# Loading the weights of a quad's four pieces one piece per row tile instead of all eight loads at once

## The chip, the cores and the metric

The kernel runs on one core of a Trainium2 chip. The metric is the device time of one execution in microseconds; the median of three runs is compared. The engines are PE (TensorE), DVE (VectorE), ACT (ScalarE), POOL (GpSimd) and SP, which here does nothing but read registers and issue DMAs.

## The reference, cut to what matters

A gated linear attention over 4 batches, 8 heads, 768 steps and 48 channels gives 3072 rows of 384 numbers. Each row then goes to one of 8 experts, picked by the largest of 8 logits, and comes back scaled by its softmax weight.

```python
for t in range(S):
    state = f[:, :, t, :, None] * state + einsum('bhd,bhe->bhde', k[:, :, t], v[:, :, t])
    y[:, :, t] = einsum('bhd,bhde->bhe', q[:, :, t], state)
x = y as (3072, 384)
logits = x @ w_gate                       # (3072, 8)
expert_idx = argmax(logits, axis=1)
for e in range(8):                        # rows of expert e
    y[rows] = maximum(x[rows] @ w1[e], 0) @ w2[e]      # 384 -> 1024 -> 384
out = gate_w[:, None] * y
```

All of it is fp32. One expert's weights are `w1` (384 x 1024) and `w2` (1024 x 384), 1536 KB each.

## The kernel before, in words

**First stage (to about 178 us).** Twelve units of attention are computed in a software pipeline. Finished rows, together with their token number and gate weight, are scattered by POOL into a table `xs` in device memory, where every expert owns a region. Near its end the first row tiles of experts 0 and 1 (`EARLY = 2`) are already worked through.

**Second stage, row tiles (lines 735 to 829).** Every expert gets three tiles of 128 rows (`TILES = 3`); two are done early, which leaves 22 tiles in the list `order` (line 305): two each of experts 0 and 1, three each of experts 2 to 7. Below, "tile i" is entry i of this list, counted from 0, and "turn i" the pass of the loop that works it. For a tile, `widen` (line 256) does 48 matmuls with `w1t` at line 263, ACT and DVE apply the ReLU, and `narrow` (line 275) does 16 matmuls with `w2t` at line 277; DVE scales by the gate weight (line 284) and POOL scatters the result to `out`. Between the two, `turn` (line 247) transposes a later tile's rows by three matmuls at line 250. Thus PE's order within a turn is: widen tile i, transpose tile i + 2, narrow tile i.

**Second stage, quads.** An expert that has more than 384 rows spills into pieces of `T = 32` rows each. Pieces of different experts are gathered four at a time into a quad, a tile of 128 rows in which every piece needs its own expert's weights. There are two quads (`QUADS = 2`). Which rows and which expert a piece has is known only at run time; `share` writes the slots into `sloti`, and SP reads each into a register (`value`, line 746). `load_quad` (line 740) issues four `qrow` loads (line 751) and then, per piece, one load of `w1` into `qw1` and one of `w2` into `qw2` (line 755); the page gives both the name `qw`. Both quads use the same buffers (`qp` has one of each). The dictionary at line 809 places them: quad 0 is worked in turn 11 and quad 1 in turn 21, the last. In such a turn the quad is transposed and widened ahead of the tile (`widen_quad`, line 770) and narrowed behind it (`narrow_quad`, line 798).

**What sets the order.** The stage is under a manual schedule: every engine executes its instructions in the order in which the program text issues them. PE, DVE, ACT, POOL and SP are all named in it. All loads of this stage are SP's, on one DMA queue. In turn i SP gets, in this order:
- `ahead("load", i + 5)` at line 813: row tile i + 4, one load of 200 KB (line 244). There are six row buffers; the load waits until tile i - 2 has been scaled at line 284.
- in a turn with a quad, after the quad has been narrowed: `load_quad` of the next quad (line 827). Its `qrow` loads wait for the scaling of the quad before.
- after the last tile of expert e: the weights of expert e + 2 (line 829), `w1t` at line 300 and `w2t` at line 302. There are two buffers of each, so they wait until that last tile has been widened and narrowed.

`load_quad(0)` stands ahead of the loop (line 810). Weights 2 are issued in turn 1 and first used by tile 4, weights 3 in turn 3 (tile 7), weights 6 in turn 12 (tile 16) and weights 7 in turn 15 (tile 19).

Of the kernel before, what the change touches and what calls it, by code (L numbers as in the profile page):

```python
# [111 lines left out]
def kernel(  # L112
# [129 lines left out]
    def load_rows(row):  # L242
        xt = rowp.tile([128, ROW], F32, name="xrow")
        nc.sync.dma_start(xt, xs[row] if isinstance(row, slice) else xs[ds(row, C)])
        return {"x": xt}
# [10 lines left out]
    def widen(x, w, hp, blocks):  # L256

        if "hT" not in x:
            x["hT"] = ep.tile([128, NF, C], F32, name="hT")
        for b in blocks:  # L260
            g, f = divmod(b, 4)
            for j in range(KD):
                nc.tensor.matmul(  # L263
                    hp[g][:, f, :],
                    lhsT=w[0][:, j, b * 128 : b * 128 + 128],
                    rhs=x["xT"][:, j, :],
                    start=j == 0,
                    stop=j == KD - 1,
                )
            if b == 3:  # L270
                nc.scalar.activation(x["hT"][:, 0:4], hp[0], AF.Relu)  # L271
            elif b == 7:
                nc.vector.tensor_scalar(x["hT"][:, 4:8], hp[1], 0.0, None, op0=OP.max)  # L273
# [8 lines left out]
    def put(x, yp, group):  # L282
        ysb = ep.tile([128, DM], F32, name="ysb")
        nc.vector.tensor_scalar(ysb, yp, x["x"][:, GATE : GATE + 1], None, op0=OP.mult)  # L284
        scatter(out, x["dst"], ysb, N - 1, group)
# [12 lines left out]
    def load_weights(e):  # L298
        w1t = wpool.tile([128, KD, F], F32, name="w1t")
        nc.sync.dma_start(w1t, moe_w1[e].rearrange("(k p) f -> p k f", p=128))  # L300
        w2t = wpool.tile([128, NF, DM], F32, name="w2t")
        nc.sync.dma_start(w2t, moe_w2[e].rearrange("(f p) d -> p f d", p=128))
        weights[e] = w1t, w2t
# [5 lines left out]
    def ahead(what, count):  # L309
        for e, t in order[done[what] : count]:  # L310
            if what == "load":
                tiles[e, t] = load_rows(slice(first[e] + t * C, first[e] + t * C + C))
            yield tiles[e, t]
        done[what] = max(done[what], min(count, len(order)))
# [405 lines left out]
    def tile_pools(st):  # L720
        pool = lambda name, bufs: st.enter_context(tc.tile_pool(name=name, bufs=bufs, space=PSUM))
        psh, pse, psz = pool("psh", 4), pool("pse", 2), pool("psz", 2)

        def banks():
            return [psh.tile([128, 4, C], F32, tag="hps", name="hps") for g in range(2)]

        def turn_late(x):
            turn(x, pse.tile([128, KD, C], F32, name="etp"))

        def narrow_late(x, w, group="out"):  # L730
            narrow(x, w, psz.tile([128, DM], F32, name="yps"), group)

        return banks, turn_late, narrow_late, psz

    with ExitStack() as st:
        banks, turn_late, narrow_late, psz = tile_pools(st)
        qp = st.enter_context(tc.tile_pool(name="qp", bufs=1))
        st.enter_context(tc.manual_schedule(engines=ordered))

        def load_quad(q):  # L740

            x = qp.tile([128, ROW], F32, name="qrow")
            w1 = qp.tile([128, 4, KD, F], F32, name="qw1")
            w2 = qp.tile([128, 4, NF, DM], F32, name="qw2")

            def value(k, g, most):
                at = sloti[0:1, k, 4 * q + g : 4 * q + g + 1]
                return nc.values_load(at, [mybir.EngineType.SP], min_val=0, max_val=most)

            for g in range(4):  # L750
                nc.sync.dma_start(x[g * T : g * T + T], xs[ds(value(0, g, NONE), T)])
            for g in range(4):
                e = value(1, g, E - 1)
                for w, src, k in ((w1, moe_w1, KD), (w2, moe_w2, NF)):
                    nc.sync.dma_start(  # L755
                        w[:, g], src[ds(e, 1)].rearrange("o (k p) f -> p (o k) f", p=128)
                    )
            return {"x": x, "w": (w1, w2)}

        def pieces():  # L760
            return [(g, slice(g * T, g * T + T)) for g in range(4)]

        def widen_quad(x):

            hp = banks()
            hq = qp.tile([128, 2, 4, C], F32, name="hq")
            for b in range(2):
                for j in range(KD):
                    for g, r in pieces():
                        nc.tensor.matmul(  # L770
                            hp[b][r].rearrange("p f c -> p (f c)"),
                            lhsT=x["xT"][:, j, r],
                            rhs=x["w"][0][:, g, j, b * 512 : b * 512 + 512],
                            start=j == 0,
                            stop=j == KD - 1,
                            skip_group_check=True,
                        )
                if b == 0:
                    nc.scalar.activation(hq[:, b], hp[b], AF.Relu)
                else:  # L780
                    nc.vector.tensor_scalar(hq[:, b], hp[b], 0.0, None, op0=OP.max)
            x["hq"] = hq

        def turn_quad(x):
            tp = banks()
            x["hT"] = qp.tile([128, NF, C], F32, name="hqT")
            for b in range(2):
                for f in range(4):
                    nc.tensor.transpose(tp[b][:, f], x["hq"][:, b, f], ident)
                (nc.scalar.copy if b == 0 else nc.vector.tensor_copy)(  # L790
                    x["hT"][:, 4 * b : 4 * b + 4], tp[b]
                )

        def narrow_quad(x):
            yp = psz.tile([128, DM], F32, name="yps")
            for f in range(NF):
                for g, r in pieces():
                    nc.tensor.matmul(  # L798
                        yp[r],
                        lhsT=x["hT"][:, f, r],  # L800
                        rhs=x["w"][1][:, g, f],
                        start=f == 0,
                        stop=f == NF - 1,
                        skip_group_check=True,
                    )
            put(x, yp, "out")


        quads = {len(order) // 2: 0, len(order) - 1: 1}
        quad = load_quad(0)  # L810
        for i, (e, t) in enumerate(order):
            w = weights[e]
            list(ahead("load", i + 5))
            if i in quads:
                turn_late(quad)
                widen_quad(quad)
            hp = banks()
            widen(tiles[e, t], w, hp, range(NF))
            if i in quads:
                turn_quad(quad)  # L820
            for x in ahead("turn", i + 3):
                turn_late(x)
            narrow_late(tiles[e, t], w)
            if i in quads:
                narrow_quad(quad)
                if quads[i] + 1 < QUADS:
                    quad = load_quad(quads[i] + 1)
            if t == TILES - 1 and e + 2 < E:
                load_weights(e + 2)

    todo = nc.values_load(fixi[0:1, 0:1], min_val=0, max_val=1)
    with tc.If(todo > 0):
# [79 lines left out]
        with ExitStack() as st:  # L912
            banks, turn_late, narrow_late, psz = tile_pools(st)
            with tc.For_i(0, E) as e:
# [10 lines left out]
                with tc.For_i(e * REGION + skip, rows_to, C) as at:  # L925
                    x = load_rows(at)
# [59 lines left out]
```

## Time and profile before

| what | us |
|---|---|
| median of 3 runs | 475.91 |
| the three runs | 472.23, 475.91, 477.03 |
| the profiled execution | 474.65 |
| its span, first to last instruction | 472.8 |
| PE busy in the span | 416.1 |
| mean granted clock of TensorE, share of full | 0.959 |

The times of single instructions below come from the profiled execution and count from the start of its span. In the timelines, a line is one instruction or a run of the same ones; the bracket at its end gives the idle time of the engine before it and what ended it. A timeline of SP shows its DMA issues; the transfer itself goes on after the issue.

### The profile page before, as it was taken

The page shows a single profiled execution, that of the slowest core. Times are in us where ns is not written, and L with a number is a line of the kernel's source. Part 1 is how long each engine was busy: PE and PEld are TensorE (multiplying, and loading weights), DVE is VectorE, ACT ScalarE, POOL GpSimd, SP SyncE. Part 2 cuts the span into 40 slices and gives each one's busy share as a digit, 9 for nine tenths or more (in the row PEclk, how much of TensorE's full clock was granted, in tenths as well). Part 3 has the DMA queues.
Part 4 walks back from the last instruction along what each step waited for, and adds up shares of the span by engine and source line. Part 5 has one row for each costly group of instructions (what it writes and reads, how often), then busy time and mean ns, then how long its engine had stood idle before and what let it go on. Part 6 is the DMA issues. An engine that isn't in the chain of part 4 may idle for free.

```text
span 472.8 us, 8470 instructions
## 1 busy us (share of the span) xinstructions
PE 416.1 (88%) x3580; PEld 336.6 (71%) x3581; DVE 159.4 (34%) x325; ACT 123.5 (26%) x172; POOL 113.7 (24%) x133
## 2 busy tenths in 40 slices
PE   0498798989898989999999999999990799999993
PEld 0488697979797877777777888576870588887471
DVE  4776748686654341211111111121110111111110
ACT  4778577878653200000000000010000001000010
POOL 4555465667461320000000110001000000000001
PEclk9979889999799999999999999999996799999997
DMA  8999755799712144999924515401899954000000
GB/s 312 406 382 383 296 215 214 268 358 377 288 71 71 71 138 166 394 397 393 389 84 148 183 36 186 168 0 40 293 398 387 357 175 180 18 17 18 17 2 20
DMA packets 42445, 98.29 MB, mean 208 GB/s; under 512 B 3440, under 2 KB 27301, under 8 KB 42400
## 3 DMA queue, kind: packets, MB, share of 16 engines
q1 hardware_dynamic: 38496, 87.48, 50.6%
q0 software_dynamic: 3200, 9.64, 5.3%
q8 instruction: 29, 0.48, 0.4%
q10 hardware_dynamic: 704, 0.56, 0.4%
q14 instruction: 16, 0.13, 0.1%
HBM read 81.43 MB, written 16.63 MB: 207 GB/s over the span
## 4 chain that ended last, share of the span: by engine, by line
PE 78%; ACT 7%; SPq 4%; DMA 4%; DVE 3%; issue 2%; POOL 1%; POOLq 0%; ACTq 0%
PE hps L263 23%; PE yps L277 22%; PE s L409 5%; PE xp L514 5%; PE yt L453 5%; SPq L755 4%; DMA xrow<-xs 3%; PE dp L469 3%; PE yt L433 3%; PE hps L770 2%; PE yps L798 2%; PE yp L277 2%; PE s L263 2%; ACT L389 2%; PE etp L250 2%
## 5 line engine op out<-in xcount | busy, mean ns | idle before, releaser
L263 PEld LDWEIGHTS hps<-xT,w1t 128*128 128x128 f32 x1056 | 121.1, 192 | 7.3 <-issue 2.3
L263 PE MATMUL hps<-xT,w1t 128*128 128x128 f32 x1056 | 121.8, 275 | 0.0
L277 PE MATMUL yps<-w2t,hT 128*128 128x384 f32 x352 | 118.3, 490 | 0.0
L277 PEld LDWEIGHTS yps<-w2t,hT 128*128 128x128 f32 x352 | 65.8, 192 | 41.3 <-issue 0.9
L161 POOL DMA_INDIRECT out_dram<-ysb,dst x26 | 25.3, 972 | 272.6 <-DVE ysb L284 272.6
L271 ACT ACTIVATE hT<-hps 128x512 f32<-128x512 f32 x22 | 13.1, 597 | 237.8 <-PE hps L263 237.8
L273 DVE TENSOR_SCALAR hT<-hps 128x512 f32<-128x512 f32 x22 | 15.2, 692 | 106.2 <-PE hps L263 101.1
L284 DVE TENSOR_SCALAR ysb<-yps,xrow 128x384 f32<-128x384 f32 x22 | 13.6, 618 | 94.3 <-PE yps L277 94.3
L409 PE MATMUL s<-q,k 64*128 64x128 f32 x384 | 29.8, 315 | 15.4 <-POOL last L392 15.4
L409 PEld LDWEIGHTS s<-q,k 64*128 64x128 f32 x384 | 27.3, 223 | 15.9 <-POOL last L392 15.0
L366 DVE TENSOR_TENSOR_SCAN r<-f,cap 128x1032 f32<-128x1032 f32 (+1 forms) x13 | 28.7, 2208 | 12.4 <-POOL f L359 12.4
L412 DVE COPY_PREDICATED at<-mpack,s 128x1024 f32<-128x1024 uint8 x24 | 30.2, 1309 | 5.8 <-PE s L409 5.7
L161 POOL DMA_INDIRECT xs<-xr,posi x24 | 24.1, 1006 | 24.4 <-DVE xr L232 7.5
L378 POOL TENSOR_TENSOR k<-k,r 128x1024 f32<-128x1024 f32 (+1 forms) x13 | 26.4, 2027 | 2.5 <-DVE r L366 2.4
L250 PE MATMUL etp<-fpack,xrow 128*128 128x128 f32 x72 | 12.2, 281 | 15.6 <-DMA xrow<-xs 15.2
L514 PE MATMUL xp<-fpack,ys 128*128 128x104 f32 x192 | 24.3, 280 | 0.7 <-ACT ys L494 0.7
L433 PE MATMUL yt<-at,v 128*64 128x128 f32 x384 | 24.1, 279 | 0.0
L514 PEld LDWEIGHTS xp<-fpack,ys 128*128 128x128 f32 x192 | 22.3, 191 | 2.2 <-ACT ys L494 1.0
L453 PE MATMUL yt<-q,state 48*48 48x128 f32 x320 | 22.5, 298 | 0.0
L433 PEld LDWEIGHTS yt<-at,v 128*64 128x64 f32 x384 | 21.2, 139 | 1.3 <-issue 0.2
L453 PEld LDWEIGHTS yt<-q,state 48*48 48x48 f32 x320 | 19.6, 133 | 1.8 <-issue 1.7
L424 PE MATMUL kp<-fpack,k 128*128 128x128 f32 x96 | 14.8, 291 | 6.5 <-ACT kn L425 3.9
(107 smaller groups left out, 364.6 us busy)
## 6 DMA issues: line engine op xcount, KB each, us to landing
qw<-in_moe_w_dram SPq DMA_DIRECT2D x16, 1536.0 KB, 9.0
w1t<-in_moe_w_dram SPq DMA_DIRECT2D x8, 1536.0 KB, 12.2
w2t<-in_moe_w_dram SPq DMA_DIRECT2D x8, 1536.0 KB, 7.9
xs<-pad SPq DMA_DIRECT2D x8, 800.0 KB, 11.1
v<-in_vu_dram SPq DMA_DIRECT2D x12, 512.0 KB, 6.9
f<-in_fu_dram SPq DMA_DIRECT2D x11, 516.0 KB, 7.9
k<-in_ku_dram SPq DMA_DIRECT2D x11, 512.0 KB, 11.5
q<-in_qu_dram SPq DMA_DIRECT2D x11, 512.0 KB
```

Of the source, the lines that this page charges most:

```text
L161: ins = nc.gpsimd.indirect_dma_start(out=dst, out_offset=bass.IndirectOffsetOnAxis(ap=idx, axis=0), in_=src, in_offset=None, bounds_check= ...
L250: nc.tensor.transpose(tp[:, j, :], x["x"][:, j * 128 : j * 128 + 128], ident)
L263: nc.tensor.matmul(hp[g][:, f, :], lhsT=w[0][:, j, b * 128 : b * 128 + 128], rhs=x["xT"][:, j, :], start=j == 0, stop=j == KD - 1,)
L277: nc.tensor.matmul(yp, lhsT=x["hT"][:, f, :], rhs=w[1][:, f, :], start=f == 0, stop=f == NF - 1)
L366: nc.vector.tensor_tensor_scan(x["r"][:, part].rearrange("p s c -> p (s c)"), x["f"][:, part].rearrange("p s c -> p (s c)"), cap[:, part]. ...
L378: nc.gpsimd.tensor_tensor(k, k, r[:, :, 1:CR], op=OP.mult)
L409: nc.tensor.matmul(ps[:, h, p], lhsT=x["k"][r, s], rhs=x["q"][r, s], start=True, stop=True)
L412: nc.vector.copy_predicated(x["at"][:, a].rearrange("p h s c -> p (h s) c"), _bc(causal, 1, SEG), ps.rearrange("p h s c -> p (h s) c"),)
L433: nc.tensor.matmul(x["yt"][r, a, p], lhsT=x["v"][:, a, 2 * p + h], rhs=x["at"][:, a, h, p], start=p == 0, stop=x["old"] is None, skip_grou ...
L453: nc.tensor.matmul(x["yt"][r, a, p], lhsT=x["old"][r, HP * a + p], rhs=x["q"][r, HP * a + p], start=False, stop=True, skip_group_check=True,)
L514: nc.tensor.matmul(xp[:, p], lhsT=x["ys"][:, a, p], rhs=wx[:, p], start=True, stop=True)
L755: nc.sync.dma_start(w[:, g], src[ds(e, 1)].rearrange("o (k p) f -> p (o k) f", p=128))
```

## The change

`load_quad` becomes a generator. Its first step allocates the quad's tiles and issues the four `qrow` loads; each further step issues the two weight loads of one piece. The loop takes the first step where `load_quad` was called before. It takes one further step in every turn that has no quad, after the turn's row load at line 813 and ahead of the turn's matmuls, until the four pieces are used up. Quad 0's pieces so belong to turns 0 to 3 and quad 1's to turns 12 to 15. No load, no matmul and no buffer is added or dropped.

```diff
--- before.py
+++ after.py
@@ -749,13 +749,14 @@
 
             for g in range(4):
                 nc.sync.dma_start(x[g * T : g * T + T], xs[ds(value(0, g, NONE), T)])
+            yield {"x": x, "w": (w1, w2)}
             for g in range(4):
                 e = value(1, g, E - 1)
                 for w, src, k in ((w1, moe_w1, KD), (w2, moe_w2, NF)):
                     nc.sync.dma_start(
                         w[:, g], src[ds(e, 1)].rearrange("o (k p) f -> p (o k) f", p=128)
                     )
-            return {"x": x, "w": (w1, w2)}
+                yield None
 
         def pieces():
             return [(g, slice(g * T, g * T + T)) for g in range(4)]
@@ -807,10 +808,13 @@
 
 
         quads = {len(order) // 2: 0, len(order) - 1: 1}
-        quad = load_quad(0)
+        coming = load_quad(0)
+        quad = next(coming)
         for i, (e, t) in enumerate(order):
             w = weights[e]
             list(ahead("load", i + 5))
+            if i not in quads:
+                next(coming, None)
             if i in quads:
                 turn_late(quad)
                 widen_quad(quad)
@@ -824,7 +828,8 @@
             if i in quads:
                 narrow_quad(quad)
                 if quads[i] + 1 < QUADS:
-                    quad = load_quad(quads[i] + 1)
+                    coming = load_quad(quads[i] + 1)
+                    quad = next(coming)
             if t == TILES - 1 and e + 2 < E:
                 load_weights(e + 2)
```

## Rows read from the trace of the kernel before

**Rows 1.** The page: its first line.
```profile
span 472.8 us, 8470 instructions
```

**Rows 2.** The page: 40 slices of 11.8 us; busy tenths, granted clock, GB/s.
```profile
PE   0498798989898989999999999999990799999993
...
PEclk9979889999799999999999999999996799999997
...
GB/s 312 406 382 383 296 215 214 268 358 377 288 71 71 71 138 166 394 397 393 389 84 148 183 36 186 168 0 40 293 398 387 357 175 180 18 17 18 17 2 20
```

**Rows 3.** The chain that ended last, in order of time: start us, us, what.
```profile
316.17 0.33 PE etp L250 x3
...
333.95 0.63 SPq L755
...
354.66 14.58 DMA xrow<-xs
369.37 0.87 PE etp L250 x3
370.25 6.20 PE yps L277 x16
...
382.13 5.16 PE yps L277 x16
```

**Rows 4.** Timeline of PE: start us, us, instructions, [idle before <-releaser].
```profile
337.84 5.52 PE L263 MATMUL hps<-xT,w1t 128*128 128x128 f32 x48
...
348.68 5.52 PE L263 MATMUL hps<-xT,w1t 128*128 128x128 f32 x48
369.37 0.87 PE L250 MATMUL etp<-fpack,xrow 128*128 128x128 f32 x3 [15.17 <-DMA xrow<-xs]
...
376.28 5.52 PE L263 MATMUL hps<-xT,w1t 128*128 128x128 f32 x48
```

**Rows 5.** Windows: stretch and length, busy us per engine, PEclk, DMA share, GB/s.
```profile
337.80:348.60 10.80, 10.80 (x68) 8.73 (x67) 1.83 (x4) 0.60 (x1) 0.97 (x1) 1.00 1.04 391
...
369.30:376.20 6.90, 6.83 (x19) 4.31 (x20) 0.62 (x2) 0.00 (x0) 0.00 (x0) 0.79 1.04 385
```

**Rows 6.** Timeline of SP's DMA issues around the second quad: start us, us, issue.
```profile
327.67 3.63 SPq L751 DMA_DIRECT2D qrow<-xs  x4
332.14 22.48 SPq L755 DMA_DIRECT2D qw<-in_moe_w_dram  x8
354.66 6.17 SPq L244 DMA_DIRECT2D xrow<-xs  x1
360.93 0.62 SPq L300 DMA_DIRECT2D w1t<-in_moe_w_dram  x1
```

**Rows 7.** DMA issues: form, KB each, median us to landing.
```profile
qw<-in_moe_w_dram SPq DMA_DIRECT2D x16, 1536.0 KB, 9.0
w1t<-in_moe_w_dram SPq DMA_DIRECT2D x8, 1536.0 KB, 12.2
...
xrow<-xs SPq DMA_DIRECT2D x24, 200.0 KB, 8.3
```

**Rows 8.** Timeline of SP's DMA issues around the first quad.
```profile
182.65 22.95 SPq L755 DMA_DIRECT2D qw<-in_moe_w_dram  x8
205.70 6.51 SPq L244 DMA_DIRECT2D xrow<-xs  x1
212.30 0.71 SPq L300 DMA_DIRECT2D w1t<-in_moe_w_dram  x1
```

**Rows 9.** Timeline of PE: starts of tiles 2 and 4 and of both quads.
```profile
205.41 5.52 PE L263 MATMUL hps<-xT,w1t 128*128 128x128 f32 x48
...
227.11 5.52 PE L263 MATMUL hps<-xT,w1t 128*128 128x128 f32 x48
...
304.38 5.36 PE L770 MATMUL hps<-qw,xT 128*32 128x512 f32 x48 [0.85 <-DVE dst L254]
...
442.38 5.36 PE L770 MATMUL hps<-qw,xT 128*32 128x512 f32 x48 [0.85 <-DVE dst L254]
```

## The prediction

> **What bounds the kernel now.** I read the page first. In the 40 slices (11.8 us each) the second half of the run has a PE digit of 9 nearly everywhere, with one hole: slice 30 shows 0 and slice 31 shows 7, the granted clock falls to 6 and 7 tenths in the same two slices, and the transfers run at 387 and 357 GB/s meanwhile [rows 2]. So the second half is bound by TensorE except for one place where TensorE stands still and the DMA queue works at full rate.
>
> The chain of waits in order of time says what that place is. It leaves the matmuls at 333.95 us for SP's queue at line 755 (the quad's weight loads), stays there until 354.66, goes on to the load of a row tile that takes 14.58 us to land, and comes back to PE at 369.37 with the transposes of that row tile [rows 3]. PE's own timeline gives the hole from its side: tile 14's widening starts at 348.68, and the next instruction, the transposes at line 250, idles 15.17 us for `xrow` [rows 4]. SP's timeline gives it from the third side: four `qrow` loads from 327.67, eight `qw` loads from 332.14 for 22.48 us, and only then, at 354.66, one `xrow` load [rows 6]. That is row tile 16, asked for in the loop's turn 12 (loads run to i + 4), transposed in turn 14 (transposes run to i + 2). It lands 354.66 + 14.58 = 369.24 us. Its issue begins the moment the eighth `qw` load is issued: SP works in program order, and the row stands behind the whole quad.
>
> **The hole's price.** Between tile starts: 348.68 − 337.84 = 10.84 us for an undisturbed tile, 376.28 − 348.68 = 27.60 us for the one with the hole [rows 4]. The excess is 16.76 us. Its parts: 15.17 us idle; the transposes then take 0.87 instead of 0.33 us (+0.54) and the narrowing 6.20 instead of 5.16 us (+1.04) [rows 3], because the granted clock is 0.79 in 369.3 to 376.2 us against 1.00 at 337.8 to 348.6 us [rows 5]; before it fell PE had stood still. 15.17 + 0.54 + 1.04 = 16.75. Bounds for the slow restart: 0 to 1.58 us; I take it all, since the clock stays at 1.00 (2.4 GHz) over the tile that has no idle time before it.
>
> **The change part by part, second quad.** Nothing is added or dropped: sixteen `qw` loads of 1536 KB and sixteen register reads stay. Only SP's order changes. At 331.3 us (327.67 + 3.63) SP has issued the four `qrow` loads [rows 6]. New order: row 16, piece 0, weights of expert 6 (two loads, the second waiting for tile 12's narrowing, which ends at 337.84 where tile 13 starts [rows 4]), row 17, piece 1, row 18, piece 2, row 19, piece 3, weights 7, row 20. Row 16 now has only the `qrow` loads ahead. Even if it needed the 14.58 us that it took behind the whole quad, it would land at about 346, and it is due when tile 14's widening ends, at 354. So the wait goes.
>
> What is late next? I price the queue by the slower of two rates. From 332.14 to row 16's landing at 369.24 are 37.1 us for eight loads of 1.573 MB and the row's 0.205 MB, 12.79 MB [rows 6, 7]: 2.90 us per MB. (The granted rate in the window at 337.8 is 391 GB/s, 2.56 us per MB [rows 5].) Tiles start every 10.85 us after 348.68; a tile's transposes come 5.36 us after its start. Counting from 332.14, with 3.15 MB for a piece or an expert:
> - row 17: 6.7 MB, lands 351.6; due in turn 15 at 364.9; 13 us to spare.
> - weights 6: before row 17; due 370.4.
> - row 18: 10.05 MB, 361.3; due 375.7.
> - row 19: 13.4 MB, 371.0; due 386.6.
> - weights 7: 19.7 MB, 389.3; due 402.9. They were issued only after tile 15 released their buffer, in either order.
> - row 20: 19.9 MB, 389.9; due in turn 18 at 397.4; 7.5 us to spare, the tightest of all (14 us at 391 GB/s).
> - piece 3: 16.6 MB, 380; due at the quad's turn, 442.38 − 16.76 = 425.6 [rows 9].
> None is late at either rate, so I take 0 for all of them.
>
> **First quad.** Eight `qw` loads from 182.65 delay row 5 to 205.70 and weights 2 to 212.30 [rows 8], yet tile 4, the first to use weights 2, starts on time at 227.11 [rows 9]. There is no hole to gain. What the change moves: pieces 0 and 1 go out at once; then SP stops at weights 2, whose buffers tile 1 frees between its widening and 205.4 (tile 2's start, [rows 9]); pieces 2 and 3 queue behind that wait, with row 6, row 7 and weights 3. Weights 2 are issued 7 us or more earlier than before, weights 3 still wait for tile 3. Pieces 2 and 3 start near 206 and, 6.3 MB at 2.90, are in by 225; the quad is due at 304.38 [rows 9]. Cost between 0 and 0: the cover is 79 us. If that cover were gone, each us late would be one us on PE.
>
> SP gets no new wait, but the pieces stand behind old ones (a row buffer, the weight buffers); behind them only rows and experts' weights wait, counted above. POOL's queue carries the output scatters and none of it moves.
>
> The Trainium skill speaks against the change: its page "DMA: Bandwidth & Descriptors" (Rules for kernel authors) says to issue a DMA early, compute, and wait late. By it, holding back six of eight loads could only lose; the rows agree for what is due soon (row 16 was the transfer issued too late) and give the pieces 45 us or more of slack, so here the rule works for the rows and costs the pieces nothing. By the rule alone the sum would be no gain and a loss wherever something ends up behind the late pieces; that is rival 3.
>
> **Sum.** The profiled execution took 474.65 us, 472.8 of it span [rows 1]. 474.65 − 16.76 = 457.9. The median of the three runs, 475.91, is 1.26 us above this execution; the same subtraction from it gives 459.15. The forecast is halfway: 458.5 us, a gain of about 3.6%.
>
> **Rivals.**
> 1. *The wait shrinks but comes back behind a later row.* Row 20, behind weights 7 and piece 3, needs better than (397.4 − 332.14) / 19.9 = 3.28 us per MB (305 GB/s). At 3.6 us per MB it lands at 403.8 and costs 6.4 us and a slow restart of up to 1.6: about 466. For it: this is the longest stretch with the queue full, 57 us without a break. Against: both rates read above are better.
> 2. *The change does not do what it says.* Nothing paces the pieces but SP's order and its buffers, so pieces 1 to 3 go out in a bunch around 338 to 350, and if row 16 were still held, for instance by the `qrow` loads' wait for the first quad's output, the hole would stay: 475.9. Against it: those four loads are through at 331.3, 23 us before the row is due.
> 3. *Slower: rows and weights 7 starve behind the late pieces.* One mechanism, at row 20 in turn 18: what used to be loaded in one stretch with nothing behind it but one row now shares the queue with every row and two experts. Below (397.4 + 16.8 − 332.14) / 19.9 = 4.12 us per MB (243 GB/s) the new hole outweighs the old one; at 4.5 us per MB (222 GB/s) row 20 lands at 421.7, 24.3 us late, and the time is 458.5 + 24.3 + 1.6 = 484. For it: rates of 71 to 215 GB/s do stand in the slices. Against: those are slices where little was asked for; where a quad loads, slices show 387 to 398 [rows 2].
>
> **How the numbers follow.** Forecast 87%, rival 1 6%, rival 2 4%, rival 3 3%. A measurement of this kernel can tell about 1% from no change: 471.2 is the line. Faster by over 1%: 87 + 6 = 93%; within 1%: 4%; slower: 3%. The three runs of before spread from 472.23 to 477.03, that is −3.7 and +1.1 about the median; around 458.5 that, and the bounds of the restart (0 to 1.6), give 454.5 on the low side. The high side takes the 459.15, the spread, and the near part of rival 1: 463. Left outside: most of rivals 1 to 3 and a little of the forecast, under 2 in 10.
>
> **What would show it right or wrong.** Right: SP's timeline after 327 shows `qrow`, then one `xrow`, then `qw` loads in pairs with `xrow` and weight loads between; PE has no idle entry for `xrow` in 340 to 400; tiles start every 10.85 us throughout; the slices have no 0 and the granted clock no dip there; SP line 755 and `xrow` leave the chain. Wrong: an idle entry at line 250 for `xrow` in a turn from 15 to 18, or at line 263 for weights 6 or 7, or at line 770 for a piece; a gain short of 15 us with no such entry would mean that the tile period itself grew under the longer transfer traffic.

## The result and the profile after

The changed kernel takes 454.75 us, median of four runs (454.02 to 458.41), against 476.47 for the kernel before beside it; the ratio is 0.957, with a 95% interval of 0.948 to 0.966. The forecast was 458.5 us, range 454.5 to 463.0. Two experiments below contain one execution each that was over 1.5% slower than the fastest of its kernel (466.29 and 485.08 us, at a mean granted clock of 0.953 and 0.936); the ratios leave these two out, and one of the kernel before (478.69 us).

The page of the changed kernel, its first line and three rows of the 40 slices, answers to [rows 1, 2]:

```profile
span 452.2 us, 8471 instructions
...
PE   0488898989898998999999999999999999999992
...
PEclk9979889999899999999999999999999999999998
...
GB/s 307 407 379 389 365 226 224 225 352 385 376 61 94 88 83 89 396 354 385 389 355 20 209 157 19 259 94 1 42 313 395 394 391 370 25 17 19 17 2 21
```

The slice with 0 and the slice with 7 are gone, and with them the 6 and 7 of the granted clock. Slices 30 to 33, where most of the second quad's weights come in, hold 370 to 395 GB/s under a PE that shows 9. The dips of the clock that are left (slices 2, 4, 5 and 10, counted from 0) lie in the first stage, but for the 8 of the last slice.

PE's timeline of the tile stage (start, length, instructions) answers to [rows 4, 9]:

```profile
179.86 5.52 PE L263 MATMUL hps<-xT,w1t 128*128 128x128 f32 x48
...
300.52 5.36 PE L771 MATMUL hps<-qw,xT 128*32 128x512 f32 x48 [0.85 <-DVE dst L254]
...
333.98 5.52 PE L263 MATMUL hps<-xT,w1t 128*128 128x128 f32 x48
...
344.82 5.52 PE L263 MATMUL hps<-xT,w1t 128*128 128x128 f32 x48
350.18 0.49 PE L250 MATMUL etp<-fpack,xrow 128*128 128x128 f32 x3
...
355.67 5.52 PE L263 MATMUL hps<-xT,w1t 128*128 128x128 f32 x48
...
421.77 5.36 PE L771 MATMUL hps<-qw,xT 128*32 128x512 f32 x48 [0.85 <-DVE dst L254]
```

Tiles 13, 14 and 15 start at 333.98, 344.82 and 355.67, 10.84 and 10.85 us apart; none of the tiles' lines carries an idle entry. The transposes of row 16 (350.18) take 0.49 us in the timeline, like any others. The chain through the same place no longer leaves PE; it answers to [rows 3]:

```profile
344.99 5.36 PE hps L263 x48
350.35 0.33 PE etp L250 x3
350.67 5.16 PE yps L277 x16
```

The windows over tiles 14 and 15 (columns as in [rows 5]) have the clock at 1.00 while the queue moves 390 GB/s or more:

```profile
344.80:355.70 10.90, 10.90 (x69) 8.75 (x68) 1.83 (x4) 0.60 (x1) 0.97 (x1) 1.00 1.05 390
355.70:366.50 10.80, 10.80 (x68) 8.70 (x67) 1.83 (x4) 0.60 (x1) 0.97 (x1) 1.00 1.05 395
```

SP's DMA issues around the second quad answer to [rows 6]:

```profile
323.81 3.63 SPq L751 DMA_DIRECT2D qrow<-xs  x4
327.49 0.42 SPq L244 DMA_DIRECT2D xrow<-xs  x1
328.73 1.02 SPq L756 DMA_DIRECT2D qw<-in_moe_w_dram  x2
329.86 0.65 SPq L300 DMA_DIRECT2D w1t<-in_moe_w_dram  x1
334.17 0.38 SPq L302 DMA_DIRECT2D w2t<-in_moe_w_dram  x1
334.60 6.86 SPq L244 DMA_DIRECT2D xrow<-xs  x1
342.24 1.09 SPq L756 DMA_DIRECT2D qw<-in_moe_w_dram  x2
343.43 6.62 SPq L244 DMA_DIRECT2D xrow<-xs  x1
350.83 1.36 SPq L756 DMA_DIRECT2D qw<-in_moe_w_dram  x2
...
359.70 2.26 SPq L756 DMA_DIRECT2D qw<-in_moe_w_dram  x2
...
370.44 6.74 SPq L244 DMA_DIRECT2D xrow<-xs  x2
```

Four `qrow` loads, then row 16 at 327.49, and only then piece 0; the last line is rows 20 and 21. The row is issued 22.7 us before it is due at 350.2; before, it was issued at 354.66 for 354. The first quad's issues answer to [rows 8]:

```profile
178.86 0.97 SPq L756 DMA_DIRECT2D qw<-in_moe_w_dram  x2
180.71 0.36 SPq L244 DMA_DIRECT2D xrow<-xs  x1
181.84 3.17 SPq L756 DMA_DIRECT2D qw<-in_moe_w_dram  x2
196.26 0.38 SPq L300 DMA_DIRECT2D w1t<-in_moe_w_dram  x1
...
203.54 1.17 SPq L756 DMA_DIRECT2D qw<-in_moe_w_dram  x2
```

Pieces 0 and 1 go out at once; SP then waits for tile 1's weight buffer until 196.26 and comes to piece 2 at 203.54. Counted from the start of tile 0, weights 2 go out after 16.4 us (196.26 − 179.86) instead of 28.6 (212.30 − 183.72).

Call the stretch from tile 0's widening to the start of the last scaling of quad 1 the tile stage. It was 464.69 − 183.72 = 280.97 us and is 444.08 − 179.86 = 264.22 us. The difference, 16.75 us, is the hole as it was priced (16.76). The profiled executions differ by 474.65 − 454.02 = 20.63 us; the other 3.86 us are in hand before tile 0 starts (183.72 against 179.86), in a stage whose program text the change does not touch. Most experiments below are about these two numbers.

### The profile page after: what moved, and what is told of

The parts are those of the page before. It is cut to its first block, busy times and chain, and to the rows that moved or that the text cites. A ratio compares the mean times of both kernels' runs of the same rounds, so it can differ in the third digit from the quotient of the medians.

```text
span 452.2 us, 8471 instructions
## 1 busy us (share of the span) xinstructions
PE 410.8 (91%) x3580; PEld 332.3 (74%) x3581; DVE 159.1 (35%) x325; ACT 123.8 (27%) x172; POOL 114.3 (25%) x133
## 4 chain that ended last, share of the span: by engine, by line
PE 86%; ACT 7%; DVE 3%; issue 2%; POOL 1%; DMA 1%; POOLq 0%; ACTq 0%
PE hps L263 26%; PE yps L277 25%; PE s L409 5%; PE xp L514 5%; PE yt L453 5%; PE dp L469 3%; PE yt L433 3%; PE s L263 2%; PE hps L771 2%; PE yps L799 2%; PE yp L277 2%; ACT L389 2%; PE kp L424 2%; PE etp L250 2%; ACT f L389 2%
## 5 line engine op out<-in xcount | busy, mean ns | idle before, releaser
L409 PE MATMUL s<-q,k 64*128 64x128 f32 x384 | 28.1, 303 | 15.5 <-POOL last L392 15.5
L409 PEld LDWEIGHTS s<-q,k 64*128 64x128 f32 x384 | 25.8, 212 | 15.9 <-POOL last L392 15.1
L397 DVE TENSOR_TENSOR q<-q,f 128x1024 f32<-128x1024 f32 (+1 forms) x13 | 14.8, 1144 | 15.0 <-ACT f L389 14.9
```

The costliest lines, as they stand in the source:

```text
L409: nc.tensor.matmul(ps[:, h, p], lhsT=x["k"][r, s], rhs=x["q"][r, s], start=True, stop=True)
```

## Experiments

Diffs are against the changed kernel unless another is named. "One look" is a single time beside a profile.

**Second quad alone.** The first quad's pieces go out at once, as before.

```diff
         quad = next(coming)
+        list(coming)
         for i, (e, t) in enumerate(order):
```

> Only the second quad's weights are spread over turns; the first quad's eight loads go out at once, as before. Theory (the whole gain is the hole for row 16 in the second quad's stretch, and the 3.86 us by which tile 0 started earlier in the changed kernel's profile is the first stage's own spread): the tile stage, from tile 0's widening to the last scaling of quad 1, is 264.2 us as in the changed kernel (281.0 before), no idle entry for a row; the time lies within 1% of the changed kernel's 454.75. Rival (spreading the first quad gives part of the gain, 3 to 4 us): tile stage or start of tile 0 later by 3 to 4 us than in the changed kernel, time near 458.5 in every run.

Measured: 457.89 us (456.32 to 459.31, four runs), ratio to the kernel before 0.962 (0.956 to 0.968). Tile stage 447.78 − 183.56 = 264.22 us, no idle entry for a row. The tile stage is as short as with both parts, so the second quad's part carries all of the hole. The time is 3.1 us above 454.75, and tile 0 starts 3.7 us later than in the changed kernel's profile (183.56 against 179.86), with the first quad loaded as before; that left the rival's 3 to 4 us standing for the first stage.

**First quad alone.** The second quad's pieces go out at once.

```diff
                     quad = next(coming)
+                    list(coming)
             if t == TILES - 1 and e + 2 < E:
```

> Only the first quad's weights are spread; the second quad's eight loads go out at once, as before. Theory: the hole stays whole, 15 us idle at line 250 for row 16 and about 1.6 us of slow restart, tile stage 281 us, one look near 472 to 479. Rival (the first quad's part carries 3 to 4 us): tile 0 starts near 180 instead of 184, or the tile stage is 277, one look near 471.

Measured: one look, 477.15 us; tile stage 467.20 − 185.45 = 281.75 us. PE's timeline:

```profile
185.45 5.52 PE L263 MATMUL hps<-xT,w1t 128*128 128x128 f32 x48
...
371.00 0.87 PE L250 MATMUL etp<-fpack,xrow 128*128 128x128 f32 x3 [15.07 <-DMA xrow<-xs]
371.67 7.28 PE L277 MATMUL yps<-w2t,hT 128*128 128x384 f32 x16
```

The hole is whole, 15.07 us. Tile 0 starts at 185.45, the latest of all profiles, with the first quad spread. The first quad's part thus gains nothing in the tile stage. The narrowing after the hole takes 7.28 us; in the kernel before it followed the transposes of [rows 4] and took 6.41:

```profile
370.04 6.41 PE L277 MATMUL yps<-w2t,hT 128*128 128x384 f32 x16
```

So the slow restart is not a fixed price.

**Only row 16 ahead, then all four pieces.**

```diff
             if i not in quads:
+                if i > min(quads):
+                    list(coming)
                 next(coming, None)
```

> First quad spread as in the changed kernel; of the second quad all four pieces go out in turn 12, right behind row 16. Theory (what counts is the bytes ahead of each row on the one queue): row 16 is on time, but row 17 now has 12.6 MB of pieces and 3.15 MB of weights 6 ahead; from the first piece at about 328.7 that is 16.1 MB or 41 to 47 us, against 361.0 when tile 15's transposes are due. A hole of 9 to 14.5 us opens at row 17, with up to 1.6 us of restart: tile stage 275 to 280. Rival (it is enough that the one late row goes first): no hole, tile stage 264.2.

Measured: one look, 474.54 us; tile stage 464.57 − 183.37 = 281.20 us. PE and SP around it:

```profile
378.51 0.88 PE L250 MATMUL etp<-fpack,xrow 128*128 128x128 f32 x3 [13.81 <-DMA xrow<-xs]
379.18 7.99 PE L277 MATMUL yps<-w2t,hT 128*128 128x384 f32 x16
```

```profile
331.00 0.42 SPq L244 DMA_DIRECT2D xrow<-xs  x1
332.24 22.28 SPq L756 DMA_DIRECT2D qw<-in_moe_w_dram  x8
354.62 6.60 SPq L300 DMA_DIRECT2D w1t<-in_moe_w_dram  x1
...
363.55 7.81 SPq L244 DMA_DIRECT2D xrow<-xs  x3
```

Row 16 was on time, and row 17 opened a hole of 13.81 us. It landed at 378.5, 46.3 us after the first piece at 332.24, with 15.93 MB issued from there up to and with the row (eight loads and weights 6 at 1.573 MB each, and the row): 2.90 us per MB, the rate that the prediction reckoned with. The idle time lies in the expected range; the stage is 1.2 us above it because the restart cost 3.17 us (281.20 − 264.22 − 13.81) instead of at most 1.6. The windows over the hole and over the restart show why:

```profile
364.70:378.50 13.80, 0.00 (x1) 0.02 (x1) 0.69 (x1) 0.00 (x0) 0.00 (x0) 0.60 1.05 392
378.50:387.00 8.50, 8.49 (x19) 5.02 (x20) 0.62 (x2) 0.00 (x0) 0.00 (x0) 0.64 0.31 122
```

The clock is 0.64 while the transposes and the narrowing run after the hole; in [rows 5] it was 0.79. So it is not enough that the late row goes first: with all four pieces ahead of row 17, the hole returns one turn later.

**The kernel before, with rows loaded two turns earlier** (diff against the kernel before):

```diff
+    late = []
...
-        xt = rowp.tile([128, ROW], F32, name="xrow")
+        xt = (late or [rowp])[0].tile([128, ROW], F32, name="xrow")
...
+        late.append(st.enter_context(tc.tile_pool(name="rowq", bufs=8)))
...
-            list(ahead("load", i + 5))
+            list(ahead("load", i + 7))
...
+    late.clear()
```

> The kernel before with its eight loads at once for either quad, but row tiles loaded two turns earlier (tile i + 6 in turn i, eight buffers of a pool of their own). Theory: rows 16 and 17 are in before the second quad's loads; row 18 and weights 6 come behind 12.6 MB. Row 18 is in time by 7 us or more; the first half of weights 6 has 14.4 MB ahead of its end, 37 to 42 us from the first piece, and is due some 38 us after it: idle 0 to 3.5 us at line 263 of tile 16, with a restart of at most 1.6; tile stage 264 to 269. Rival (not the rows' place in the queue but the full-rate transfer itself holds PE): the hole stays near 15 us, tile stage near 281.

Measured: one look, 463.17 us; tile stage 453.21 − 183.40 = 269.81 us. PE's timeline at tile 16 (the edit shifts the widening to line 265):

```profile
373.94 7.22 PE L265 MATMUL hps<-xT,w1t 128*128 128x128 f32 x48 [3.72 <-DMA w1t<-in_moe_w_dram]
```

The hole for the row is gone although both quads go out at once; in its place tile 16 waits 3.72 us for weights 6, and its widening takes 7.22 instead of 5.52 us. The weights' first half ends 42.1 us after the first piece (331.82 to 373.94) as the last of 14.36 MB (eight loads, a row and this half): 2.93 us per MB. Idle time and stage lie just above the expected ends (3.5 and 269). A full-rate transfer does not hold PE; the place in the queue does.

**Two pieces per turn.**

```diff
                 next(coming, None)
+                if i > min(quads):
+                    next(coming, None)
```

> First quad as in the changed kernel; of the second quad two pieces in turn 12 and two in turn 13. Theory: row 17 has 9.8 MB to go, 25 to 28.5 us from 328.7, in by 357, due 361.0: no wait. Row 18 has all four pieces ahead, 16.3 MB, 42 to 47 us, in at 370.4 to 376, due 371.9: idle 0 to 4 us at line 250 in turn 16, tile stage 264.2 to 269.5. Rival (one piece per turn is needed): a hole at row 17 already, of 5 us or more.

Measured: one look, 463.56 us; tile stage 453.62 − 183.00 = 270.62 us. PE's timeline at tile 16:

```profile
378.77 0.87 PE L250 MATMUL etp<-fpack,xrow 128*128 128x128 f32 x3 [3.59 <-DMA xrow<-xs]
379.44 7.63 PE L277 MATMUL yps<-w2t,hT 128*128 128x384 f32 x16
```

Row 17 was in time, row 18 was 3.59 us late, 46.9 us after the first piece as the last of 16.14 MB (the pieces and weights 6, rows 17 and 18): 2.91 us per MB. The idle time is within the expected 0 to 4; the stage is 1.1 us beyond the range, since the restart after so short a hole cost 2.81 us (270.62 − 264.22 − 3.59).

**Piece ahead of the row in every turn.**

```diff
-            list(ahead("load", i + 5))
             if i not in quads:
                 next(coming, None)
+            list(ahead("load", i + 5))
```

> In every turn the piece's two loads go out ahead of the turn's row load instead of behind it. Theory (bytes ahead count, not the order within a turn): row 16 has 3.35 MB to go, in by 338.5, due 350.2; rows 17, 18 and 19 have 9.6, 12.9 and 16.3 MB, in by 357, 366 and 376, due 361.0, 371.9 and 382.7. No hole, tile stage 264.2. Rival (the rows must go ahead of their turn's piece): idle entries for rows 16 or 17 of some 5 to 9 us, tile stage 270 or more.

Measured: one look, 458.48 us; tile stage 448.54 − 184.32 = 264.22 us. SP's issues in turns 12 and 13:

```profile
332.74 1.03 SPq L756 DMA_DIRECT2D qw<-in_moe_w_dram  x2
333.82 1.40 SPq L244 DMA_DIRECT2D xrow<-xs  x1
...
339.77 7.49 SPq L756 DMA_DIRECT2D qw<-in_moe_w_dram  x2
347.30 6.80 SPq L244 DMA_DIRECT2D xrow<-xs  x1
```

Row 16 goes out behind piece 0, row 17 behind piece 1, and nothing waits. So the order within a turn is not what does it: in this kernel and in the changed one at most one piece comes between two rows, and that was enough.

**The changed kernel again.** No edit.

> The changed kernel unaltered, for the size of the gain. Theory: tile stage 264.2 us again, while tile 0 starts anywhere from 179 to 185 us, as the granted clock falls in the first stage; span minus the slow-clock time (span times one minus the mean granted clock) is the same in all runs, near 442 us. The gain against the kernel before is 16.8 us plus or minus the first stage's spread: ratio 0.960 to 0.967. Rival (the change also shortens the first stage by 3 to 4 us): tile 0 at 180 us in every run, ratio 0.957 or less.

Measured: 454.99 us (453.92 to 460.2, six runs) against 475.62 (eleven runs), ratio 0.959 (0.954 to 0.964). Tile stage 445.63 − 181.41 = 264.22 us. The six spans times their mean granted clock are 441.9 to 443.5 us, while the spans run from 452.1 to 458.4: most of the runs' spread is time at the lower clock. Tile 0 starts at 181.41 here. The ratio's middle lies just below the theory's 0.960 to 0.967 and above the rival's 0.957, so this run did not decide where the extra 3 to 4 us come from. But the rival wanted an early tile 0 in every run, and the run of 460.2 us does not have it: in the profiles with this tile stage the span is 272.3 us longer than the start of tile 0 (452.2 − 179.86, 453.7 − 181.41), so its span of 458.4 us puts tile 0 near 186. The three experiments that follow bear on the same question.

**First quad's pieces in turns 4 to 7.**

```diff
-            if i not in quads:
+            if i not in quads and i > 3:
                 next(coming, None)
```

> The changed kernel, but the first quad's pieces go out in turns 4 to 7 instead of 0 to 3. Theory (the 3 to 5 us that the changed kernel gains beyond the hole are the first stage's own clock, which no part of the change reaches): tile stage 264.2 us, no idle entry for rows, weights or pieces; tile 0 starts anywhere from 179 to 186 us, median time anywhere from 454 to 459. Rival (the change shortens the first stage): tile 0 near 180 to 181 us, median 454 to 456.

Measured: 457.70 us median of six runs (453.96 to 466.29), ratio 0.961 (0.955 to 0.968). Tile stage 448.50 − 184.28 = 264.22 us; tile 0 starts at 184.28. Two of its runs are near 454 us, three between 457 and 459, and one took 466.29, with a span of 464.4 us at a mean granted clock of 0.953: 442.6 as a product, like the others (441.7 to 442.2). The pieces may thus go out four turns later at no cost, and a kernel with the change can have the long first stage.

**The kernel before with w2 ahead of w1** (diff against the kernel before):

```diff
-                for w, src, k in ((w1, moe_w1, KD), (w2, moe_w2, NF)):
+                for w, src, k in ((w2, moe_w2, NF), (w1, moe_w1, KD)):
```

> The kernel before with the two loads of a piece in the other order, w2 ahead of w1. Theory: hole at row 16 of 15 us and a restart of 1.6 to 3.2, tile stage 280.8 to 282.5 us; the first stage's program is unaltered, yet its clock may fall elsewhere: tile 0 from 179 to 186 us, median time 471 to 478. Rival (the first stage is long in every kernel that loads the second quad at once): tile 0 at 183.5 us or later, median 475 to 477.

Measured: 473.80 us (471.77 to 485.08, twelve runs), ratio to the kernel before 1.000 (0.996 to 1.004). Tile stage 463.44 − 181.47 = 281.97 us with 15.25 us idle for row 16:

```profile
367.21 0.87 PE L250 MATMUL etp<-fpack,xrow 128*128 128x128 f32 x3 [15.25 <-DMA xrow<-xs]
```

Tile 0 starts at 181.47 in this profile and the median is below 475 us; the rival excluded both.

**First quad alone, again.** The edit is that of "First quad alone".

> Only the first quad's weights are spread, the second quad's go out at once. Theory: same time as before within its spread, ratio 0.99 to 1.01, tile stage 280.8 to 282.5 us. Rival (spreading the first quad shortens the first stage by 3 to 4 us): median 471 to 472.5, ratio near 0.992.

Measured: 475.50 us (470.95 to 476.92), ratio 1.002 (0.999 to 1.005). PE's timeline:

```profile
179.29 5.52 PE L263 MATMUL hps<-xT,w1t 128*128 128x128 f32 x48
...
364.82 0.87 PE L250 MATMUL etp<-fpack,xrow 128*128 128x128 f32 x3 [15.05 <-DMA xrow<-xs]
```

Tile stage 461.02 − 179.29 = 281.73 us, hole 15.05 us, and tile 0 starts at 179.29: earlier than in the changed kernel's own profile (179.86), with the hole whole. The same kernel had tile 0 at 185.45 in its first run. The two profiles' windows from 120 to 132 us, first run and second run, show one of the places:

```profile
120.00:132.00 12.00, 10.49 (x108) 9.47 (x108) 7.85 (x18) 6.54 (x9) 5.58 (x6) 0.63 0.62 227
```

```profile
120.00:132.00 12.00, 10.70 (x160) 9.67 (x160) 9.04 (x19) 8.81 (x13) 6.84 (x8) 1.00 0.57 201
```

Same code, a granted clock of 0.63 in one and 1.00 in the other; PE gets through 108 matmuls in the first window and 160 in the second. So the start of tile 0 moves by up to 6.2 us between profiles of one and the same kernel, early starts occur with the hole (179.29, 181.47) and late ones without it (184.28, 184.32). An early start does not need the change. But that is not to say that the change has no part in it: eight of the ten runs of the changed kernel came out below 456 us, and only two of eleven runs of the other kernels with the same tile stage. Neither quad's part by itself, nor later pieces, brought the early start as a rule, and nothing tried here sets where the clock falls. Of the 21.7 us between the two medians (476.47 − 454.75) the experiments thus show the 16.75 to 17.75 us of the hole; the cause of the other 4 to 5 us stays open.

## Why the prediction was right, point by point

**The hole and its cause** held as told: row 16 stood behind the second quad on SP's one queue. The tile stage is 16.75 us shorter where 16.76 was the forecast; loading the second quad at once brings the hole back, and loading rows earlier removes the wait for row 16 without touching the quad.

**What is late next** was priced at 2.90 us per MB, and three experiments that made something late measured 2.90, 2.91 and 2.93. None of the seven items on the list was late. The tightest, row 20, was forecast to land 57.8 us after the first piece with 7.5 us to spare. In the changed kernel it was issued at 370.44 and landed 14.9 us later, at 385.3: 56.6 us after the first piece, and 8.2 us before its transposes at 393.57. Rival 1's wait did not come. The rate of rival 3 (4.1 us per MB and more) did not occur.

**The first quad** is worth nothing either way: tile stages of 264.22 us with its pieces at once, in turns 0 to 3 or in turns 4 to 7.

**The slow restart** was bounded by 0 and 1.58 us from a single execution. That bound was too tight: as tile stage less 264.22 less idle time it cost 1.87 us after the wait for weights 6, 2.81 and 3.17 us after the holes at rows 18 and 17, and in the three later executions with the hole at row 16 the tile stage was 281.73 to 281.97 us, that is 17.5 to 17.75 above 264.22. The usual price of the hole is so 0.8 to 1 us above the term in the sum.

**The step that was mis-sized** is the last of the sum, from the profiled execution to the median of the runs: halfway between two subtractions gave 458.5, the measured median is 3.75 us lower. By the figures above about 1 us of it can be the restart. The rest lies in the first stage, which was shorter in most runs of the changed kernel for a reason that stays open, and which the sum held at no change. The range allowed for the spread of the runs before, and the measured median sits 0.25 us inside its low end: that the median fell inside is luck in part, since no term of the sum forecast a shorter first stage.

The Trainium skill's rule that was weighed, to issue a DMA early (its page "DMA: Bandwidth & Descriptors", Rules for kernel authors), fits the rows here: issued two turns earlier they shortened the tile stage by 11.2 us (280.97 to 269.81). For the pieces no run shows a gain from it: issued four turns later the first quad's cost nothing, and issued all at once the second quad's cost 17 us.

## What to carry to other kernels

On one in-order queue a large load that is needed late delays every small one that is issued behind it. For each load, add up the bytes ahead of it, multiply by the rate read from the trace and compare with the time at which its reader stands ready; then spread the bulk load so that no row has more ahead of it than its slack allows. Here one piece between two rows was enough, and two pieces per turn were already too many.

## What the runs showed of the hardware that was not expected

A transfer behind a full queue landed at 2.90 to 2.93 us per MB, counted from the first piece, while the windows show 394 GB/s (2.54 us per MB) once the transfers are under way: for 12.79 MB that is 37.1 us against 32.5. The kernel before shows two parts of this difference in the windows over its hole, up to row 16's landing:

```profile
332.14:335.00 2.86, 2.86 (x15) 1.93 (x14) 1.22 (x3) 0.00 (x0) 0.00 (x0) 1.00 0.51 118
335.00:369.24 34.24, 19.20 (x125) 15.70 (x123) 3.14 (x6) 1.19 (x2) 1.94 (x2) 0.84 1.04 394
```

The first 2.9 us after the first piece's issue run at 118 GB/s, which loses some 2 us. The rest is other bytes: the two windows moved 13.8 MB, 1.0 MB more than the eight loads and the row. POOL's scatters of finished tiles (0.2 MB each, at 338.93 and 349.78) are among them; what else was moved is not shown. So 2.90 us per MB is an average over a stretch of this length, start and other traffic included, and as such it served for the due times here.

After PE had stood still, the lower clock cost between 1.6 and 3.2 us, and not in proportion to the idle time: 3.59 us idle cost 2.81 us, 15.17 us idle cost 1.58 us in one execution and 15.05 to 15.25 us idle cost 2.46 to 2.50 us in three others.
